# The attention gate of a diffusion transformer block: from TensorE to VectorE, ScalarE and GpSimd

## Chip, core and metric

One core of a Trainium2 chip. Its engines run their own instruction queues side by side and meet at semaphores: TensorE (matrix products, into PSUM), VectorE, ScalarE, GpSimd (element-wise work), and SyncE, which only issues transfers here. In profile rows they are PE, DVE, ACT, POOL and SP; PEld is TensorE's loading of weights. The metric is the device time of one execution in microseconds (us), the median over runs.

## What is computed

One block over two images of 256 tokens, D = 1152, two heads. A small vector c per image is turned into six vectors per image by `w_mod`: shift, scale and gate for the attention half and for the MLP half. The change concerns `gate_a`.

```python
mod = (_silu(c) @ w_mod).reshape(B, 6, 1, D)
shift_a, scale_a, gate_a, shift_m, scale_m, gate_m = [mod[:, i] for i in range(6)]
h = _layernorm(x, axis=-1) * (1 + scale_a) + shift_a
qkv = (h @ wqkv).reshape(B, N, 3, H, Dh)
...
attn = _softmax(jnp.einsum('bqhd,bkhd->bhqk', q, k) * Dh ** (-0.5), axis=-1)
a = jnp.einsum('bhqk,bkhd->bqhd', attn, v).reshape(B, N, D) @ wo
x = x + gate_a * a
h2 = _layernorm(x, axis=-1) * (1 + scale_m) + shift_m
m = _gelu(h2 @ w_fc1) @ w_fc2
return x + gate_m * m
```

All inputs are bf16; sums run in fp32.

## The kernel before

Tokens are four tiles of 128 (two per image). Contractions over D run over nine slices of 128 (`kt` 0 to 8). All SBUF is one tensor, `arena`, cut by byte offsets, so nearly every profile row names `arena` and `psum`, and several buffers share space over time. The stages in TensorE's order: layernorm and scale of x; k; `sh` (the shift vector, 36 narrow products); q; scores and softmax of the four (image, head) pairs, between the pieces of v; transposes of the probabilities; `rows` (three modulation vectors); the rest of v; probabilities times v (`PV`); `wo` with gate, residual and second layernorm; fc1 with gelu; fc2 with the second gate.

**Order.** The code records units with reads, writes and an estimated length. `Sched.schedule` (L281) fixes the order. TensorE (`pe`) and SyncE (`sp`) keep the order in which units are recorded. For VectorE, ScalarE and GpSimd a list scheduler runs the units with their estimated lengths and takes, of the units that are ready, the one with the longest chain behind it. `emit` (L398) writes one in-order queue per engine, with the semaphore waits that are still needed. An instruction that waits therefore holds up all that stand behind it on its engine. The estimates know nothing of engines that hinder each other.

**The attention gate before.** `ld_modr0`, `3` and `6` (L891-892) load 2592 KB each: for three kt, the 3 x 1152 columns of gate_a, shift_m and scale_m. They stand on SyncE's queue behind V's weights (`ld_wv`, L890), which wait until `sh` has freed their place. `rows` (L977) takes silu(c), two columns per kt, as the stationary operand, and streams the 27 x 128 columns in four groups of 32 columns side by side (`quad_mm`, L880): two sets of four instructions per kt, of 448 and 416 columns. ScalarE copies the gate part to bf16 `ROWS` (L982), VectorE transposes the rest into `MT` (L985), GpSimd's queue stores the gate to a scratch tensor in DRAM and loads it back spread over all 128 partitions as `GA[0]` and `GA[1]` (L988-992).

**Who reads it.** `wo_tile` (L1055): VectorE multiplies each finished PSUM piece by `GA[b]` (`wo_t1`, L1067), GpSimd adds x (`wo_x1`, L1068), VectorE takes the layernorm statistics (L731 and on), GpSimd the power -0.5 (L735), VectorE a product of two columns (`nmr2`, L1072), ScalarE normalises (`xn2`, L1073), TensorE transposes (`xn2_T`, L1078), and fc1 follows.

**The attention stage.** `q_kt0` to `q_kt8` (L1105) fill six PSUM banks, which `qk_ev` units copy out, on VectorE and ScalarE in turn; `S_halves` (L921) and `s_and_softmax` (L931) use those banks again. Per pair: scores on TensorE (`S_b_h`), `smax` and `snb` on VectorE (L943, L944), two `sexp` on ScalarE (L947), `sri` and the normalisation `spn` on VectorE (L949, L951), whose number is 2b + h. `pt_transposes` (L953) needs `spn`, and `PT_ev` copies its result out. V's pieces (`v_t_ci`, L965) use three banks in turn, copied out by `v_ev`.

**The MLP gate** is already made off TensorE: `mlp_gate` (L994) runs 18 multiply-adds on VectorE (weights times a per-partition scalar plus accumulator, L999 and L1002), a transpose in blocks of 32 (L1006), a reduction (L1008) and small moves and adds (L1011-1017).

Of the kernel before, what the change touches and what calls it, by code (L numbers as in the profile page):

```python
# [492 lines left out]
F32 = mybir.dt.float32  # L493
ALU = mybir.AluOpType
ACTF = mybir.ActivationFunctionType
AX = mybir.AxisListType

P = 128
NTOK = 512
D = 1152  # L500
KT = 9
# [16 lines left out]
def c_act(n, aps=0):  # L518
    return 190.0 + 0.8 * n + 75.0 * aps


def c_dve_psum32(n):
    return 110.0 + 1.13 * n


def c_dve_psum16(n):
    return 110.0 + 0.57 * n
# [14 lines left out]
def build_kernel(nc, x, c, wqkv, wo, w_mod, w_fc1, w_fc2, out):  # L542
    S = Sched()
# [3 lines left out]
    scratch = scratch_t.ap()  # L547
    with (
# [4 lines left out]
        def sb(off, nbytes, dt=BF16):  # L553
            assert off % 4 == 0 and off + nbytes <= ARENA_BYTES, (off, nbytes)
            v = arena[:, off // 2:(off + nbytes) // 2]
            if dt == F32:
                v = v.bitcast(F32)
            return v

        def ps32(bank, c0=0, n=512):  # L560
            return psum[:, bank * 512 + c0: bank * 512 + c0 + n]
# [7 lines left out]
        W1 = 20736  # L569
        O_A, O_B, O_C, O_R = 0, W1, 2 * W1, 3 * W1  # L570
# [10 lines left out]
        def misc(nbytes):  # L581
            o = mo[0]
            mo[0] += (nbytes + 3) // 4 * 4
            assert mo[0] <= ARENA_BYTES
            return o

        def wmat(o, f):
            return sb(o, KT * f * 2).rearrange("p (k f) -> p k f", k=KT)
# [7 lines left out]
        WMODR = wmat(O_R + W1, 3 * D)  # L596
# [18 lines left out]
        GA = [sb(O_GA + b * 2304, 2304) for b in range(2)]  # L615
        GM = [sb(o + 18432, 2304) for o in (O_A, O_C)]
        XN2 = [sb(O_R + 4 * W1 - (i + 1) * 2304, 2304) for i in range(4)]
        ROWS = sb(O_R + 4 * W1 - 5 * 2304, 2304)[:, 0:288]
        T1 = [sb(O_X + i * 1536, 1536, F32) for i in range(3)]
        OST = [sb(O_X + 4608 + i * 768, 768) for i in range(3)]  # L620
        gt_offs = ([O_P + i * 1024 for i in range(8)] + [O_B + i * 1024 for i in range(20)]
# [11 lines left out]
        ST32 = sb(misc(72), 72, F32)  # L633
# [4 lines left out]
        MT = sb(misc(2304), 2304, F32)  # L638
# [21 lines left out]
        wmod_v = w_mod.rearrange("(k p) f -> p k f", p=P)  # L660
# [4 lines left out]
        def dma(dst, src, nbytes, name, is_out=False, eng="sp", run=4096):  # L665
            eff = 1.0 if run >= 4096 else (1.08 if run >= 2304 else (1.15 if run >= 1536 else (1.3 if run >= 1024 else 1.42)))
            return S.op(eng, 500.0 if eng == "sp" else 150.0, lambda e: e.dma_start(dst, src), reads=[src], writes=[dst],  # L667
                        name=name, dma_bytes=nbytes * eff, is_out=is_out)

        def dve(cost, fn, reads, writes, name):  # L670
            return S.op("dve", cost, fn, reads=reads, writes=writes, name=name)

        def act(cost, fn, reads, writes, name):
            return S.op("act", cost, fn, reads=reads, writes=writes, name=name)

        def pool(cost, fn, reads, writes, name):
            return S.op("pool", cost, fn, reads=reads, writes=writes, name=name)

        def copy_on(eng, dst, src, n, psum16, name):
            if eng == "act":  # L680
                act(c_act(n), lambda e: e.activation(out=dst, in_=src, func=ACTF.Copy), [src], [dst], name)  # L681
            else:
                dve(c_dve_psum16(n) if psum16 else c_dve_psum32(n), lambda e: e.tensor_copy(dst, src), [src], [dst], name)  # L683

        def mm(o, l, r, st, sp, **kw):
            S.instr(lambda e: e.matmul(o, lhsT=l, rhs=r, start=st, stop=sp, **kw), reads=[l, r], writes=[o])  # L686
# [8 lines left out]
        for (ka, kb) in ((0, KC), (KC, KT)):  # L695
            w = (kb - ka) * P
# [49 lines left out]
        for t in range(4):  # L746
# [3 lines left out]
            else:  # L750
# [3 lines left out]
                                                                                 op0=ALU.subtract, op1=ALU.mult),  # L754
# [122 lines left out]
        def quads(w, g0, g1, q):  # L877
            return w.rearrange("p (g q c) -> p g q c", q=4, c=32)[:, g0:g1, q, :]

        def quad_mm(bank, w, g0, g1, kt):  # L880
            n = 32 * (g1 - g0)
            for q in range(4):
                o = psum[32 * q:32 * q + 2, bank * 512:bank * 512 + n].rearrange("p (g c) -> p g c", c=32)
                mm(o, ST[:, kt:18:9], quads(w, g0, g1, q), kt == 0, kt == KT - 1, tile_position=(0, 32 * q))
# [2 lines left out]
        S.unit("pe", KT * 4 * 31.0 + 100.0, "sh")  # L887
        for kt in range(KT):
            quad_mm(0, WSH[:, kt, :], 0, 9, kt)
        dma(WV, wqkv_v[:, :, 2 * D:3 * D], D * D * 2, "ld_wv", run=2304)  # L890
        for k0 in range(0, KT, 3):  # L891
            dma(WMODR[:, k0:k0 + 3, :], wmod_v[:, k0:k0 + 3, 2 * D:5 * D], 3 * P * 3 * D * 2, "ld_modr%d" % k0)
        MT1 = ps32(0, 0, 288)
        dve(c_dve_psum32(288), lambda e: e.transpose(SHA, MT1), [MT1], [SHA], "sha")  # L894
        for kt in range(KT):
            for b in range(2):
                src, dst = HK[:, kt, b * 256:(b + 1) * 256], HX[:, kt, b * 256:(b + 1) * 256]
# [74 lines left out]
            copy_on("act" if v_rr[0] % 2 else "dve", V[:, t, ci * CH:(ci + 1) * CH], o, CH, False, "v_ev%d_%d" % (t, ci))  # L972


        row_parts = ((3, 0, 14), (4, 14, 27))

        def rows():  # L977
            S.unit("pe", KT * 864 / 2.4 + 500.0, "rows")
            for kt in range(KT):
                for bank, g0, g1 in row_parts:  # L980
                    quad_mm(bank, WMODR[:, kt, :], g0, g1, kt)
            copy_on("act", ROWS, ps32(3, 0, 288), 288, False, "rows_ev")  # L982
            for i, (bank, c0, n, d0) in enumerate(((3, 288, 160, 0), (4, 0, 416, 160))):
                src, dst = ps32(bank, c0, n), MT[:, d0:d0 + n]
                dve(c_dve_psum32(n), lambda e, src=src, dst=dst: e.transpose(dst, src), [src], [dst], "mt_%d" % i)  # L985
            sc, so = MT[:, 288:576].rearrange("p (k r) -> p k r", r=32)[:, :, 0:2], SC1M.rearrange("p (k b) -> p k b", b=2)
            dve(170, lambda e: e.tensor_scalar(out=so, in0=sc, scalar1=1.0, scalar2=None, op0=ALU.add), [sc], [so], "sc1m")
            for b in range(2):  # L988
                dma(scratch[0, b].rearrange("(k q c) -> q k c", q=4, c=32), ROWS[b:128:32, :].rearrange("p (k c) -> p k c", c=32),
                    2304, "st_g%d" % b, eng="pool")  # L990
            for b in range(2):
                dma(GA[b], scratch[0, b].partition_broadcast(P), P * D * 2, "ld_g%d" % b, eng="pool")

        def mlp_gate(prev):  # L994
# [55 lines left out]
        def acc_bank():  # L1050
            b = acc[acc_rr[0] % len(acc)]
            acc_rr[0] += 1
            return b
# [47 lines left out]
            act(c_act(ntok), lambda e: e.activation(out=dst, in_=o, func=ACTF.Gelu_apprx_tanh), [o], [dst], "gelu_%d_%d" % (f, tok0))  # L1101


        qb = (2, 3, 4, 5, 6, 1)
        for kt in range(KT):  # L1105
            S.unit("pe", KG * c_mm(512), "q_kt%d" % kt)
# [21 lines left out]
        pt_transposes(1, 1)  # L1128
        v_proj(2, 0)
        rows()  # L1130
        wfc1_load(0)
        wfc1_load(1)
# [38 lines left out]
        for t in range(4):  # L1171
            b = t // 2
# [3 lines left out]
            for (c0, c1) in pieces:  # L1176
                w = c1 - c0
                S.unit("pe", JT * c_mm(w), "fc2_%d_%d" % (t, c0))
                o = ps32(acc_bank(), 0, w)
# [22 lines left out]
def bass_standalone__dit_block__diffusion_kernel(  # L1202
    nc: bass.Bass,
    x: bass.AP,
    c: bass.AP,
    wqkv: bass.AP,
    wo: bass.AP,
    w_mod: bass.AP,
    w_fc1: bass.AP,
    w_fc2: bass.AP,  # L1210
    out: bass.AP,
):
    build_kernel(nc, x, c, wqkv, wo, w_mod, w_fc1, w_fc2, out)
# [28 lines left out]
```

## Time and profile before

| | |
|---|---|
| median of three runs | 246.35 us (246.02 to 246.6) |
| the profiled execution | 246.26 us |
| its span, first to last instruction | 244.2 us |
| granted TensorE clock | 1.000 |
| TensorE busy | 239.3 us, 98% of the span |
| VectorE, ScalarE, GpSimd busy | 98.7, 63.0, 21.5 us |
| transfers | 51.57 MB |

The busy shares in 40 slices of 6.1 us, and what the transfers moved:

```profile
PE   7999999999999999999999999999999999999995
...
DVE  3742450446323689879999600000022222111112
ACT  5730340235312306983322333222000000000000
POOL 1400000000021275600000110000000000000000
DMA  6999999999994999979943589200000000000000
```

Each digit is the busy share in tenths. TensorE is full from the second slice to the last. GpSimd does nothing from slice 3 to slice 11, and VectorE is half idle there. In later fences a row of groups has line, engine, operation, shapes and count, then busy us and mean ns of one, then the idle time before it and what ended that. A row of a timeline has start, duration, engine, line, operation and count, and in brackets the idle time before it and its releaser.

### The profile page before, as it was taken

What the parts mean: (1) busy time and instruction counts of PE and PEld (TensorE: products, weight loads), DVE (VectorE), ACT (ScalarE), POOL (GpSimd) and SP (SyncE); (2) the same over time, 40 slices, a digit from 0 to 9 for tenths busy, and PEclk for the clock granted to TensorE, in tenths of its full rate; (3) what the DMA queues carried; (4) which work ended last, traced back from release to release, by engine and by line L of the source; (5) the groups of instructions that cost most, each with busy time, mean ns of one, the idle gap of its engine ahead of it and who ended that gap; (6) DMA issues with size and microseconds to landing.
All of it is one profiled execution on the core that took longest, in us unless ns stands there. A gap on an engine that the chain in (4) does not pass through costs nothing.

```text
span 244.2 us, 3973 instructions
## 1 busy us (share of the span) xinstructions
PE 239.3 (98%) x1721; PEld 146.8 (60%) x1731; DVE 98.7 (40%) x205; ACT 63.0 (26%) x128; POOL 21.5 (9%) x37
## 2 busy tenths in 40 slices
PE   7999999999999999999999999999999999999995
PEld 2689844466557666798544444444565656566575
DVE  3742450446323689879999600000022222111112
ACT  5730340235312306983322333222000000000000
POOL 1400000000021275600000110000000000000000
DMA  6999999999994999979943589200000000000000
GB/s 244 350 377 393 389 381 401 419 422 406 387 329 111 341 386 391 392 246 396 349 132 101 172 256 393 79 0 3 0 16 16 19 17 16 19 16 16 29 22 16
DMA packets 28875, 51.57 MB, mean 211 GB/s; under 512 B 1587, under 2 KB 15675, under 8 KB 28859
## 3 DMA queue, kind: packets, MB, share of 16 engines
q1 hardware_dynamic: 28384, 50.14, 56.9%
q0 software_dynamic: 448, 1.19, 2.0%
q8 instruction: 13, 0.21, 0.4%
q14 instruction: 3, 0.02, 0.0%
q10 hardware_dynamic: 27, 0.00, 0.0%
HBM read 50.14 MB, written 1.19 MB: 210 GB/s over the span
## 4 chain that ended last, share of the span: by engine, by line
PE 97%; ACT 1%; issue 0%; DVE 0%; POOL 0%; POOLq 0%
PE psum L686 95%; PE psum L689 2%; ACT arena L1091 1%; ACT arena L1073 1%; DVE arena L792 0%; POOL arena L709 0%; DVE arena L1184 0%; DVE arena L1185 0%; POOL arena L708 0%; DVE arena L783 0%; POOL arena L713 0%; POOLq L1227 0%
## 5 line engine op out<-in xcount | busy, mean ns | idle before, releaser
L686 PE MATMUL psum<-arena 128*128 128x384 bf16 (+9 forms) x1632 | 236.1, 312 | 2.2 <-POOL arena L709 1.4
L686 PEld LDWEIGHTS psum<-arena 128*128 128x128 bf16 (+1 forms) x1642 | 141.4, 97 | 92.3 <-issue 5.0
L1184 DVE TENSOR_TENSOR arena<-psum,arena 128x384 f32<-128x384 f32 (+3 forms) x14 | 7.0, 501 | 89.4 <-PE psum L686 89.4
L1101 ACT ACTIVATE arena<-psum 128x512 bf16<-128x512 f32 (+1 forms) x44 | 22.5, 522 | 42.6 <-PE psum L686 42.6
L681 ACT ACTIVATE arena<-psum 128x512 bf16<-128x512 f32 (+6 forms) x28 | 14.8, 549 | 40.1 <-PE psum L686 38.2
L683 DVE CAST arena<-psum 128x512 bf16<-128x512 f32 (+2 forms) x21 | 13.0, 627 | 26.5 <-PE psum L686 26.3
L1002 DVE SCALAR_TENSOR_TENSOR arena<-arena 128x1152 f32<-128x1152 bf16 x16 | 21.3, 1409 | 0.0
L1068 POOL TENSOR_TENSOR arena<-arena 128x384 f32<-128x384 f32 x12 | 11.0, 914 | 12.9 <-DVE arena L1067 11.7
L667 POOL DMA_DIRECT2D dit_scratch<-arena x4 | 2.6, 662 | 94.0 <-ACT arena L681 58.7
L731 DVE BATCH_NORM_STATS2 arena<-arena 128x6 f32<-128x384 f32 (+1 forms) x18 | 9.5, 549 | 1.2 <-DMA arena<-in_x_dram 1.1
L1073 ACT ACTIVATE arena<-arena 128x1152 bf16<-128x1152 f32 x4 | 5.4, 1353 | 9.5 <-DVE arena L1072 9.5
L1067 DVE TENSOR_TENSOR arena<-psum,arena 128x384 f32<-128x384 f32 x12 | 6.6, 548 | 3.2 <-PE psum L686 3.0
L689 PEld LDWEIGHTS psum<-arena 128*128 128x128 bf16 (+1 forms) x89 | 6.0, 98 | 2.4 <-DMA arena<-in_c_dram 0.8
L689 PE MATMUL psum<-arena 128*128 128x128 bf16 (+1 forms) x89 | 7.3, 219 | 0.1
L1185 DVE TENSOR_TENSOR arena<-arena 128x384 bf16<-128x384 f32 (+3 forms) x14 | 7.0, 501 | 0.5
L1091 ACT ACTIVATE arena<-psum,arena 128x128 bf16<-128x128 bf16 x16 | 6.1, 460 | 3.2 <-PE psum L689 2.5
L1088 DVE TENSOR_SCALAR arena<-psum,arena 128x128 bf16<-128x128 bf16 x20 | 5.5, 336 | 2.0 <-PE psum L689 1.8
L943 DVE TENSOR_REDUCE arena<-psum 128x2 f32<-128x512 f32 x4 | 2.8, 692 | 4.0 <-PE psum L686 3.7
L947 ACT ACTIVATE arena<-psum,arena 128x256 bf16<-128x256 f32 x8 | 3.7, 470 | 2.4 <-DVE arena L944 1.9
L735 POOL TENSOR_TENSOR arena<-arena 128x1 f32<-128x1 f32 x6 | 3.3, 555 | 6.1 <-DVE arena L734 6.1
L792 DVE TENSOR_SCALAR arena<-psum,arena 128x256 bf16<-128x256 bf16 x7 | 2.4, 348 | 3.6 <-PE psum L689 2.3
L900 ACT ACTIVATE arena<-arena 128x256 bf16<-128x256 bf16 x6 | 2.5, 495 | 3.3 <-DVE arena L894 3.3
(46 smaller groups left out, 43.1 us busy)
## 6 DMA issues: line engine op xcount, KB each, us to landing
arena<-in_w_mod_dram SPq DMA_DIRECT2D x4, 2592.0 KB, 20.2
arena<-in_w_fc_dram SPq DMA_DIRECT2D x9, 1152.0 KB, 8.2
arena<-in_w_fc_dram SPq DMA_DIRECT2D x4, 2592.0 KB, 17.4
arena<-in_wqkv_dram SPq DMA_DIRECT2D x18, 288.0 KB, 10.2
arena<-in_w_mod_dram SPq DMA_DIRECT2D x3, 864.0 KB, 13.2
arena<-in_wqkv_dram SPq DMA_DIRECT2D x1, 2592.0 KB, 10.9
arena<-in_wo_dram SPq DMA_DIRECT2D x1, 2592.0 KB, 32.7
arena<-in_w_mod_dram SPq DMA_DIRECT2D x3, 480.0 KB, 6.8
```

The lines of the kernel that those rows point to most:

```text
L681: act(c_act(n), lambda e: e.activation(out=dst, in_=src, func=ACTF.Copy), [src], [dst], name)
L683: dve(c_dve_psum16(n) if psum16 else c_dve_psum32(n), lambda e: e.tensor_copy(dst, src), [src], [dst], name)
L686: S.instr(lambda e: e.matmul(o, lhsT=l, rhs=r, start=st, stop=sp, **kw), reads=[l, r], writes=[o])
L689: S.instr(lambda e: e.transpose(o, i_, idn), reads=[i_, idn], writes=[o])
L731: dve(550, lambda e, s=s, o=o: e.bn_stats(out=o, in_=s), [s], [o], "bn_%s_%d" % (tag, ci))
L1002: u = dve(1300, lambda e, o=o, w=w, s1=s1: e.scalar_tensor_tensor(out=o, in0=w, scalar=s1, in1=o, op0=ALU.mult, op1=ALU.add), [w, s1, o], ...
L1068: S.op("pool", 930, lambda e, xs=xs, x1c=x1c: e.tensor_tensor(out=x1c, in0=x1c, in1=xs, op=ALU.add), reads=[x1c, xs], writes=[x1c], name=" ...
L1073: act(1344, lambda e: e.activation(out=xn2, in_=x1, func=ACTF.Identity, scale=rs, bias=nm), [x1, rs, nm], [xn2], "xn2_%d" % t)
L1091: act(440, lambda e, o=o, dst=dst, s1=s1, s2=s2: e.activation(out=dst, in_=o, func=ACTF.Identity, scale=s1, bias=s2), [o, s1, s2], [dst], ...
L1101: act(c_act(ntok), lambda e: e.activation(out=dst, in_=o, func=ACTF.Gelu_apprx_tanh), [o], [dst], "gelu_%d_%d" % (f, tok0))
L1184: dve(c_dve_psum32(w), lambda e, o=o, gm=gm, t1=t1: e.tensor_tensor(out=t1, in0=o, in1=gm, op=ALU.mult), [o, gm], [t1], "fc2_t1_%d_%d" % ( ...
L1185: dve(c_dve_32(w), lambda e, t1=t1, x1c=x1c, ost=ost: e.tensor_tensor(out=ost, in0=t1, in1=x1c, op=ALU.add), [t1, x1c], [ost], "fc2_out_%d ...
```

## The change

`gate_a` is no longer part of `rows`. Its weights are loaded by three transfers of their own (`ld_ga0`, `3`, `6`, 864 KB each), which stand ahead of V's weights on SyncE's queue; `ld_modr` shrinks to 1728 KB each. A new function `attn_gate`, recorded ahead of q, computes, with weights as bf16 and the accumulators as fp32 in a part of the arena that is free at that time:

- image 0: nine VectorE instructions of 128 x 1152 (`ga_0_kt`): one product, eight multiply-adds into `ACCA[:, 0]`;
- image 1: nine ScalarE products (`gp_kt`), the first into `ACCA[:, 1]`, the others in turn into two buffers; eight GpSimd adds (`ga_1_kt`) into `ACCA[:, 1]`;
- per image on VectorE a transpose (`ga_T`), a reduction (`ga_red`), three moves, three adds, a cast (`ga_bf`) and a small transpose (`ga_t`); then two stores on GpSimd's queue (`st_ga`), and at the end the load `ld_g` of `GA[b]` as before.

`ga_T0` writes into the buffer of odd products, so it waits for the GpSimd add of kt 7; `ga_T1` waits for that of kt 8. The buffers lie where the MLP gate's weights (`ld_gm`) come later, which now wait for the stores. `rows` keeps shift_m and scale_m: two sets of 288 columns per kt, and no copy on ScalarE.

```diff
-        ROWS = sb(O_R + 4 * W1 - 5 * 2304, 2304)[:, 0:288]
+        ACCA = sb(O_R, 9216, F32).rearrange("p (b d) -> p b d", b=2)
+        ACTA = sb(O_R + 9216, 9216, F32).rearrange("p (b d) -> p b d", b=2)
+        GPA = sb(O_R + 18432, 1152, F32).rearrange("p (q g) -> p q g", q=4)
...
+        for k0 in range(0, KT, 3):
+            dma(WMODR[:, k0:k0 + 3, 0:D], wmod_v[:, k0:k0 + 3, 2 * D:3 * D], 3 * P * D * 2, "ld_ga%d" % k0, run=2304)
         dma(WV, wqkv_v[:, :, 2 * D:3 * D], D * D * 2, "ld_wv", run=2304)
         for k0 in range(0, KT, 3):
-            dma(WMODR[:, k0:k0 + 3, :], wmod_v[:, k0:k0 + 3, 2 * D:5 * D], 3 * P * 3 * D * 2, "ld_modr%d" % k0)
+            dma(WMODR[:, k0:k0 + 3, D:3 * D], wmod_v[:, k0:k0 + 3, 3 * D:5 * D], 3 * P * 2 * D * 2, "ld_modr%d" % k0)
...
-        row_parts = ((3, 0, 14), (4, 14, 27))
+        row_parts = ((3, 9, 18), (4, 18, 27))
...
-            copy_on("act", ROWS, ps32(3, 0, 288), 288, False, "rows_ev")
...
+        def attn_gate():
+            for kt in range(KT):
+                o, w, s1 = ACCA[:, 0, :], WMODR[:, kt, 0:D], ST32[:, kt:kt + 1]
+                if kt == 0:
+                    dve(1300, lambda e, o=o, w=w, s1=s1: e.tensor_scalar(out=o, in0=w, scalar1=s1, scalar2=None, op0=ALU.mult),
+                        [w, s1], [o], "ga_0_%d" % kt)
+                else:
+                    dve(1410, lambda e, o=o, w=w, s1=s1: e.scalar_tensor_tensor(out=o, in0=w, scalar=s1, in1=o, op0=ALU.mult, op1=ALU.add),
+                        [w, s1, o], [o], "ga_0_%d" % kt)
+                s1 = ST32[:, 9 + kt:10 + kt]
+                o = ACCA[:, 1, :] if kt == 0 else ACTA[:, kt % 2, :]
+                act(c_act(D, 1), lambda e, o=o, w=w, s1=s1: e.activation(out=o, in_=w, func=ACTF.Copy, scale=s1), [w, s1], [o], "gp_%d" % kt)
+                if kt > 0:
+                    a_ = ACCA[:, 1, :]
+                    pool(3000, lambda e, o=o, a_=a_: e.tensor_tensor(out=a_, in0=a_, in1=o, op=ALU.add), [a_, o], [a_], "ga_1_%d" % kt)
+            pool(100, lambda e: e.memset(GBA, 0.0), [], [GBA], "gba0")
+            lin = scratch[0].rearrange("b (g c) -> b g c", c=32)
             for b in range(2):
...
+                a_, t_ = ACCA[:, b, :], ACTA[:, 1 - b, :]
+                gp, gb, gt = GPA[:, :, 36 * b:36 * b + 36], GBA[:, 64 * b:64 * b + 64], GTA[:, 64 * b:64 * b + 64]
+                dve(1400, lambda e, a_=a_, t_=t_: e.transpose(t_, a_), [a_], [t_], "ga_T%d" % b)
+                t3, o = t_.rearrange("p (g r) -> p g r", r=32), gp[:, 0, :]
+                dve(1400, lambda e, t3=t3, o=o: e.tensor_reduce(out=o, in_=t3, axis=AX.X, op=ALU.add), [t3], [o], "ga_red%d" % b)
...
+                dma(lin[b, 0:32], gt[:, 0:32], 2048, "st_ga%d_0" % b, eng="pool")
+                dma(lin[b, 32:36], gt[0:4, 32:64], 256, "st_ga%d_1" % b, eng="pool")
                 dma(GA[b], scratch[0, b].partition_broadcast(P), P * D * 2, "ld_g%d" % b, eng="pool")
...
+        attn_gate()
         qb = (2, 3, 4, 5, 6, 1)
```

On the queues the change has these places. VectorE: `ga_0_0` to `ga_0_4` before the copies of q (`qk_ev2`, `4`, `0`, `6`), `ga_0_5` and `ga_0_6` before `smax_0` and `qk_ev8`, `ga_0_7` before `sri_0` and `spn_0`, `ga_0_8` before `sri_2`, `smax_3` and `spn_2`; then `spn_1`, `v_ev1_0`, `PT_ev0`, `ga_T0`, `sri_3`, `v_ev1_2`, `spn_3`. GpSimd: the eight adds one after the other, then the stores and loads. ScalarE: four products before the copies of q, the others between copies and exps.

## The prediction

> **What bounds the kernel now.** I read the chain of waits first, then the groups by shape, then the timelines of GpSimd and VectorE. In the chain, whose shares are of the 244.2 us span, TensorE holds nearly everything:
>
> ```profile
> PE 97%; ACT 1%; issue 0%; DVE 0%; POOL 0%; POOLq 0%
> ```
>
> So work taken off TensorE is a gain of its full length, and work put on another engine is free until TensorE has to wait for it. From 45 to 65 us (attention) TensorE takes what VectorE makes. Starts and durations in us, VectorE and TensorE:
>
> ```profile
> 44.97 2.63 DVE L683 CAST arena<-psum 128x512 bf16<-128x512 f32 x4 [10.54 <-PE psum L686]
> 50.38 0.69 DVE L943 TENSOR_REDUCE arena<-psum 128x2 f32<-128x512 f32 x1 [2.77 <-PE psum L686]
> ...
> 61.68 0.69 DVE L951 TENSOR_TENSOR arena<-arena 128x512 bf16<-128x512 bf16 x1
> ...
> 64.19 0.39 PE L689 MATMUL psum<-arena 128*128 128x128 bf16 x4
> ```
>
> The casts free q's banks (S_halves follows at 48.8, S_0_0 at 49.3); L951 is the last softmax normalisation, spn_3, and at 64.19 TensorE transposes its result (PT_1_1). GpSimd is idle from 11.5 to 70.3 us, so nothing here shows what happens when GpSimd and VectorE work together. A later stage does:
>
> ```profile
> 95.05 0.92 POOL L1068 TENSOR_TENSOR arena<-arena 128x384 f32<-128x384 f32 x1
> ...
> 95.43 0.55 DVE L1072 SCALAR_TENSOR_TENSOR arena<-arena 128x1 f32<-128x1 f32 x1
> ...
> 99.34 0.91 POOL L1068 TENSOR_TENSOR arena<-arena 128x384 f32<-128x384 f32 x1
> ...
> 99.62 0.64 DVE L1072 SCALAR_TENSOR_TENSOR arena<-arena 128x1 f32<-128x1 f32 x1
> ...
> 103.44 0.16 DVE L1072 SCALAR_TENSOR_TENSOR arena<-arena 128x1 f32<-128x1 f32 x1 [0.66 <-POOL arena L735]
> ```
>
> One element per partition takes 0.16 us with GpSimd idle, but 0.55 and 0.64 beside a GpSimd add, ending at 95.98 and 100.26 where the adds end at 95.97 and 100.25 (a third, at 90.96, takes 0.63 and ends 0.01 after its add). This VectorE instruction reads two operands from SBUF. Those with one (L731, L1067, L1088) keep their length beside the same adds. I read an exclusive port: the second comer waits for the whole of the first. Each ga_0 multiply-add (weights and accumulator), each L951 and each new GpSimd add reads two operands from SBUF.
>
> **The change, part by part.**
>
> *TensorE.* The pass at lines 979-981 streams 864 columns per kt, starts at 65.97 and is followed at 69.36: 3.39 us. The pass with 288 columns (sh) has nine steps of 0.122 us, 1.1 us in all, so 576 columns take 2.2 to 2.3. Gain 1.1 us. The ScalarE eviction that goes (0.41 us) was in idle time.
>
> *Transfers.* The three 864 KB pieces of gate weights go ahead of V's on SP's queue, without a wait. V's 2592 KB landed at 42.4 (issue 31.47 plus 10.9) at about 390 GB/s, 6.7 us, so it began at 35.7; the pieces now land at 38.0, 40.2 and 42.5, and V's at 49.2. Its first use is at 53.0: 3.8 us of cover, beyond which a delay would count in full. The later loads carry the same total of bytes and keep their times. ld_gm now waits on SP for the gate's stores (about 91.5 us) with the fc2 loads behind it; the two fc1 loads ahead of it, 11.3 us of transfer in the old trace, cover this. Cost nothing.
>
> *Prices.* VectorE multiply-add 1.4 (L1002, 1409 ns). ScalarE product: between 1.15 (L739) and 1.35 (L1073), taken 1.2 as its input is bf16. GpSimd add of 1152: the same instruction at 384 takes 914 ns, so 2.74 if all scales; a GpSimd cast of 18 columns takes 0.19, so with that as fixed part 2.36; with the 0.56 of L735 (a power, 1 column) as fixed part 1.63. I take 2.6. GPSIMD Engine Reference, section 3.1, of the Trainium skill has 4497 ns for an fp32 add of 2048 elements; from that I estimate 2.53, and the sum would be 0.5 lower.
>
> *The stage, in the order that the planner writes for the changed kernel.* ga_0_0 to ga_0_2 run 38.0 to 41.5; gp_1 is done at 40.4, so add 1 waits at the port and has it next: the multiply-add behind must first see its predecessor's semaphore, and the same holds for GpSimd, so they alternate. Port: add 1 41.5-44.1, ga_0_3 -45.5, add 2 -48.1, ga_0_4 -49.5. Queued on VectorE behind ga_0_4 are the four q casts, 4.5 us late: S_halves 50.9, S_0_0 51.5 (+2.2). Port: add 3 -52.1, ga_0_5 -53.5, add 4 -56.1, ga_0_6 -57.5, add 5 -60.1. Behind ga_0_6 stand smax_0 and the cast qk_ev8, so S_0_1 starts at 58.9, not 54.46 (+4.4). Then ga_0_7 60.1-61.5, spn_0 61.8-62.5, add 6 -65.1, ga_0_8 -66.5, add 7 -69.1, spn_2 -69.8, add 8 -72.4, spn_1 -73.1. PT_1_0 waits for spn_2: 69.9, not 60.81 (+9). Then VectorE alone: v_ev1_0 0.56, PT_ev0 0.42, ga_T0 1.29 (half of L1006), sri_3 0.15, v_ev1_2 0.56, spn_3 0.69, with semaphores 76.7. PT_1_1 starts at 76.75 instead of 64.19: 12.55 us late.
>
> The account is simple: from 41.5 the port carries 8 adds (20.8), 6 multiply-adds (8.4) and 3 normalisations (2.1), 31.3 us and 0.3 idle, ending at 73.1. Which goes first moves the early stalls, not this sum; only if spn_1 gets in before add 8 is it 2.6 less. ScalarE's nine products (10.8 us) stay below it: by this count an exp waits at most 0.2 for one, and off the path.
>
> SBUF — State Buffer of the Trainium skill, section "Who interferes with whom", states this lock for a VectorE instruction with two SBUF inputs against a GpSimd one that reads SBUF, whole instructions long; the trace agrees at 384 columns and shows no longer one. By that rule the sum stands as it is; without it, see the first rival.
>
> *After the stage.* The reduction chain (two reduces 1.28, one transpose 1.29, 14 small ones near 0.2, L1011 and L1014) ends near 84.5 for image 0 and 86.5 for image 1. GpSimd issues four stores, the last to 87.9; they land about 4.2 after issue (the 2.2 KB stores at 70.3), image 0's by 89.5, and ld_g0 4.1 to 4.7 after its own: GA 0 is there at 93.5 to 94.2. Its first reader, wo_t1_0_0, moves from 82.71 to 94.2; ld_g1 behind it on GpSimd's queue waits for image 1's stores (91.5), and wo_x1, queued behind that, comes at 94.8. Cost nothing, though the cover is at most 0.7 us: the loads near 140 us took 7.1, and so late a GA 0 would cost up to 2 us, as xn2T_0 has only 1.2 to spare. All behind it is bound by TensorE and shifts as a whole.
>
> *Sum.* 246.26 (the profiled execution, 2.06 of it outside the span) + 12.55 - 1.1 = 257.7. The median, 246.35, is 0.1 above that execution: 257.8.
>
> **Rivals.**
>
> *No lock between long instructions* (the other side). It would show at 41.5, where add 1 and ga_0_3 would run together. Adds follow each other from 40.4 at 2.6 each; add 7 ends at 61.7, ga_T0 at 63.0, and no cast is late. What stays is that v_ev1_2 now stands ahead of spn_3: V's block ends at 64.19, the cast 0.56 and spn_3 0.69 follow, PT_1_1 starts at 65.5 (+1.3). 246.35 + 1.3 - 1.1 = 246.6, no change; 245.3 if even that is hidden. For it: no row has both long. Against it: three short ones out of three ended with the add. It decides where the overlap is over half of each add.
>
> *A lighter add.* At 1.63, eight adds are 7.8 shorter: 250.0. At 2.74, 258.9. With spn_1 ahead of add 8: 255.2.
>
> *A colder TensorE.* The 17 warm-up matmuls of 512 columns at the start take 0.38 each, later 49 take 10.74, 0.22 each. The longest new pause is 4.5 us, before PT_1_0. If it brings the slow pace back for as long as at the start (5.7 us), 5.7 x (1 - 0.22/0.38) = 2.4, partly hidden under the next wait: 259 to 260.2. Against it: the granted clock reads 1.00 in every window, so only matmul spacing would show it. TensorE: Matmul & The Clock Gate of the Trainium skill, Part 1, has the clock halved after an idle window of about 3.4 us that runs freely; a 4.5 us pause need not cover one.
>
> *A late gate vector*: +2, 259.8.
>
> **How the numbers follow.** The lock with adds of 2.36 to 2.74, either order: 0.67 (255 to 259). Lighter adds or a looser lock: 0.13 (249.5 to 255). Cold clock or late gate: 0.11 (259 to 262). No lock: 0.08; anything else 0.01. The range 250 to 261 leaves out the no-lock case and the ends of two others, under 0.2. About 0.2% (0.5 us) is what a measurement can tell from no change. No lock splits into same 0.05, faster 0.02 and slower 0.01, which with the rest gives slower 0.92; 0.01 more of faster is for what I overlook.
>
> **What would show it.** In the changed profile: GpSimd adds near 2.6 back to back with multiply-adds, each of which seems to last up to 4 us; L951 rows over 2 us; TensorE pauses before S_halves, S_0_1, PT_1_0, PT_0_1 and PT_1_1; the rows pass 2.2 us; wo_t1_0_0 waiting for TensorE, not a DMA. Multiply-adds of 1.4 beside adds of 2.6 that overlap them would make the forecast wrong.

## The result, and the profile after

The changed kernel takes 256.52 us (median of six runs, 255.43 to 256.94) where the kernel before takes 246.47 (six runs, 245.92 to 246.87): ratio 1.0405, 95% interval 1.0387 to 1.0422. The forecast was 257.8. The profiled execution took 256.89 us, its span is 254.8 (244.2 before), the mean granted clock 0.987.

The page of the changed kernel, the chain that ended last, as shares of the span:

```profile
PE 76%; DVE 13%; DMA 8%; ACT 1%; SPq 1%; issue 0%
```

TensorE held 97% of it before. VectorE now holds 13%. Of the 8% for transfers 11.45 us stand where that stretch begins: the first product, `ga_0_0` at 37.46, waits for its weights, and from there the chain runs through VectorE. What TensorE waited for (us in total, times, longest):

```profile
PE psum L693 <- DVE arena L957: 6.1, 2, 4.8
PE psum L690 <- DVE arena L687: 1.9, 2, 1.2
```

L957 is `spn` (L951 before), L687 the copies out of PSUM (L683 before). The timeline of TensorE has the places:

```profile
49.83 6.25 PE L690 MATMUL psum<-arena 64*128 64x256 bf16 x45 [0.68 <-DVE arena L687]
57.25 4.52 PE L690 MATMUL psum<-arena 128*128 128x256 bf16 x31 [1.17 <-DVE arena L687]
...
68.25 0.61 PE L693 MATMUL psum<-arena 128*128 128x128 bf16 x4 [4.80 <-DVE arena L957]
...
71.54 0.63 PE L693 MATMUL psum<-arena 128*128 128x128 bf16 x4
...
75.84 0.40 PE L693 MATMUL psum<-arena 128*128 128x128 bf16 x4 [1.25 <-DVE arena L957]
```

These are `S_halves` (48.75 before), the rest of `S_0_1` (54.78), `PT_1_0` (60.81), `PT_0_1` (62.50) and `PT_1_1` (64.19): +1.1, +2.5, +7.4, +9.0 and +11.65. Of the last, `rows` gives back 1.08 (2.31 us instead of 3.39), and 10.6 us is what the span grew by. GpSimd and VectorE in the same stretch, one timeline each:

```profile
39.94 18.52 POOL L1008 TENSOR_TENSOR arena<-arena 128x1152 f32<-128x1152 f32 x5 [28.54 <-ACT arena L1005]
61.21 9.46 POOL L1008 TENSOR_TENSOR arena<-arena 128x1152 f32<-128x1152 f32 x3 [2.74 <-ACT arena L1005]
```

```profile
41.23 3.65 DVE L1001 SCALAR_TENSOR_TENSOR arena<-arena 128x1152 f32<-128x1152 bf16 x1
...
57.11 1.38 DVE L950 TENSOR_SCALAR arena<-arena 128x2 f32<-128x2 f32 x1
...
59.01 1.40 DVE L1001 SCALAR_TENSOR_TENSOR arena<-arena 128x1152 f32<-128x1152 bf16 x1
...
60.41 0.14 DVE L950 TENSOR_SCALAR arena<-arena 128x2 f32<-128x2 f32 x1
60.52 0.69 DVE L957 TENSOR_TENSOR arena<-arena 128x512 bf16<-128x512 bf16 x1
...
65.76 2.44 DVE L957 TENSOR_TENSOR arena<-arena 128x512 bf16<-128x512 bf16 x1
...
68.19 2.50 DVE L950 TENSOR_SCALAR arena<-arena 128x2 f32<-128x2 f32 x1
70.61 0.68 DVE L957 TENSOR_TENSOR arena<-arena 128x512 bf16<-128x512 bf16 x1
```

Five adds follow each other every 3.70 us (18.52 / 5). A multiply-add takes 1.40 when GpSimd pauses (59.01) and 3.65 when an add is ahead of it; `spn` takes 0.69 or 2.44. Even `snb` (L950), two elements per partition, takes 0.14 or 2.50. Nobody is slower at the work; the second comer waits for the first. "The port" below stands for what the two engines lock against each other.

### The profile page after: what moved, and what is told of

The parts are those of the page before. It is cut to its first block, busy times and chain, and to the rows that moved or that the text cites. A ratio compares the mean times of both kernels' runs of the same rounds, so it can differ in the third digit from the quotient of the medians.

```text
span 254.8 us, 4051 instructions
## 1 busy us (share of the span) xinstructions
PE 241.8 (95%) x1731; PEld 147.3 (58%) x1731; DVE 130.4 (51%) x234; ACT 73.1 (29%) x136; POOL 49.4 (19%) x48
## 4 chain that ended last, share of the span: by engine, by line
PE 76%; DVE 13%; DMA 8%; ACT 1%; SPq 1%; issue 0%
PE psum L690 74%; DMA arena<-in_w_mod_dram 8%; DVE arena L1001 7%; PE psum L693 2%; DVE arena L957 1%; DVE arena L687 1%; DVE arena L950 1%; DVE arena L949 1%; ACT arena L1127 1%; SPq L671 1%; ACT arena L1109 1%; DVE arena L998 0%; DVE arena L796 0%; DVE arena L1221 0%; DVE arena L1222 0%
## 5 line engine op out<-in xcount | busy, mean ns | idle before, releaser
L690 PE MATMUL psum<-arena 128*128 128x384 bf16 (+7 forms) x1642 | 237.6, 311 | 4.0 <-DVE arena L687 1.9
L1008 POOL TENSOR_TENSOR arena<-arena 128x1152 f32<-128x1152 f32 x8 | 27.1, 3390 | 32.2 <-ACT arena L1005 31.3
L1038 DVE SCALAR_TENSOR_TENSOR arena<-arena 128x1152 f32<-128x1152 bf16 x16 | 21.4, 1415 | 0.0
L685 ACT ACTIVATE arena<-psum 128x512 bf16<-128x512 f32 (+5 forms) x27 | 14.2, 554 | 24.4 <-PE psum L690 20.9
L687 DVE CAST arena<-psum 128x512 bf16<-128x512 f32 (+2 forms) x21 | 12.9, 624 | 11.3 <-PE psum L690 11.2
L1001 DVE SCALAR_TENSOR_TENSOR arena<-arena 128x1152 f32<-128x1152 bf16 x8 | 18.0, 2253 | 0.2
L1005 ACT ACTIVATE arena<-arena 128x1152 f32<-128x1152 bf16 x9 | 11.1, 1255 | 6.8 <-POOL arena L1008 4.7
L671 POOL DMA_DIRECT2D dit_scratch<-arena x6 | 3.4, 570 | 49.1 <-DVE arena L1053 35.3
L953 ACT ACTIVATE arena<-psum,arena 128x256 bf16<-128x256 f32 x8 | 3.7, 472 | 11.2 <-DVE arena L950 11.2
L950 DVE TENSOR_SCALAR arena<-arena 128x2 f32<-128x2 f32 x4 | 5.7, 1419 | 0.0
```

The source lines that it names most:

```text
L1001: dve(1410, lambda e, o=o, w=w, s1=s1: e.scalar_tensor_tensor(out=o, in0=w, scalar=s1, in1=o, op0=ALU.mult, op1=ALU.add), [w, s1, o], [o], ...
L1005: act(c_act(D, 1), lambda e, o=o, w=w, s1=s1: e.activation(out=o, in_=w, func=ACTF.Copy, scale=s1), [w, s1], [o], "gp_%d" % kt)
L1008: pool(3000, lambda e, o=o, a_=a_: e.tensor_tensor(out=a_, in0=a_, in1=o, op=ALU.add), [a_, o], [a_], "ga_1_%d" % kt)
L1038: u = dve(1300, lambda e, o=o, w=w, s1=s1: e.scalar_tensor_tensor(out=o, in0=w, scalar=s1, in1=o, op0=ALU.mult, op1=ALU.add), [w, s1, o], ...
```

## The experiments

Ratios are to the kernel before, run beside it on the same chip (its median lay between 246.38 and 247.0), with 95% intervals. In every run but a1 the orders of VectorE, ScalarE and GpSimd are written out by hand; in e1 to e4b, e6, e8 and e10 they stand as in the changed kernel, but for the moves shown.

| kernel | us | ratio |
|---|---|---|
| e1 adds of 16 columns | 246.94 | 1.0025 (1.0014 to 1.0037) |
| e2 multiply-adds of 16 columns | 250.16 | 1.0165 (1.0150 to 1.0180) |
| e3 as e1, spn_3 ahead | 245.50 | 0.9966 (0.9956 to 0.9975) |
| e4, e4b idle matmuls in the pause | 256.50, 256.63 | 1.0424 (1.0408 to 1.0439), 1.0398 (1.0374 to 1.0421) |
| a1 the changed kernel again | 256.09 | 1.0394 (1.0363 to 1.0424) |
| e5 another split of the work | 249.21 | 1.0079 (1.0047 to 1.0110) |
| e6 adds in three pieces | 254.50 | 1.0314 (1.0291 to 1.0337) |
| e7 e5 mended | 247.88 | 1.0043 (1.0028 to 1.0059) |
| e8 e6, spn_3 ahead | 251.56 | 1.0186 (1.0152 to 1.0221) |
| e9 e7 mended | 245.34 | 0.9951 (0.9938 to 0.9965) |
| e10 changed kernel, spn_3 ahead | 255.11 | 1.0352 (1.0335 to 1.0368) |

### One side of the alternation made short: e1, e2, e3

e1: all instructions and waits stay, only the length of the GpSimd adds goes.

```diff
-                    a_ = ACCA[:, 1, :]
+                    a_, o = ACCA[:, 1, 0:16], o[:, 0:16]
```

> The changed kernel with its order of instructions kept, but each of GpSimd's eight adds covers 16 of 1152 columns; image 1's gate lacks the rest of the sum. Port theory: with the adds short nothing blocks VectorE; the multiply-adds take 1.41 us each one after the other, the normalisations 0.69; the only pause left is the one before PT_1_1, since v_ev1_2 stands ahead of spn_3 (1.3 us), and rows gain 1.1: 246.6 us, between 246.0 and 247.5. Rival, the added work itself (18 operations more on VectorE, nine products on ScalarE, V's weights later) makes attention late: still 251 us or more.

Measured 246.94, as expected, with `PT_1_1` at 65.71. All but some 0.6 us of the loss of 10 hangs on the adds' length. The lock works the other way round too; GpSimd's timeline of e1:

```profile
47.88 1.24 POOL L1008 TENSOR_TENSOR arena<-arena 128x16 f32<-128x16 f32 x1 [3.85 <-ACT arena L1005]
50.79 0.22 POOL L1008 TENSOR_TENSOR arena<-arena 128x16 f32<-128x16 f32 x1 [1.66 <-ACT arena L1005]
```

The same 16 columns take 0.22 alone and 1.24 behind a multiply-add that had begun at 47.63.

e2: the same for VectorE's multiply-adds, the adds whole.

```diff
-                    dve(1410, lambda e, o=o, w=w, s1=s1: e.scalar_tensor_tensor(out=o, in0=w, scalar=s1, in1=o, op0=ALU.mult, op1=ALU.add),
-                        [w, s1, o], [o], "ga_0_%d" % kt)
+                    o, ws = o[:, 0:16], w[:, 0:16]
+                    dve(1410, lambda e, o=o, w=ws, s1=s1: e.scalar_tensor_tensor(out=o, in0=w, scalar=s1, in1=o, op0=ALU.mult, op1=ALU.add),
+                        [ws, s1, o], [o], "ga_0_%d" % kt)
```

> The changed kernel with its order kept and the eight adds whole, but VectorE's eight multiply-adds cover 16 of 1152 columns; image 0's gate lacks the rest. Port theory: adds of 2.5 us follow each other without pause, VectorE's short two-operand operations and its scalings (snb) still wait for the add that runs, the normalisations above all; by hand PT_1_1 is 5 us late: 250.4 us, between 249 and 252. Rival, the long multiply-adds load VectorE too much and the adds are harmless: 246.6 us.

Measured 250.16, as expected. VectorE's timeline of e2, then GpSimd's group of rows from 36 to 76 us:

```profile
40.21 0.23 DVE L1002 SCALAR_TENSOR_TENSOR arena<-arena 128x16 f32<-128x16 bf16 x1 [0.97 <-DMA arena<-in_w_mod_dram]
40.66 2.35 DVE L1002 SCALAR_TENSOR_TENSOR arena<-arena 128x16 f32<-128x16 bf16 x1 [0.21 <-DVE arena L1002]
...
60.18 2.55 DVE L957 TENSOR_TENSOR arena<-arena 128x512 bf16<-128x512 bf16 x1
```

```profile
L1009 POOL TENSOR_TENSOR arena<-arena 128x1152 f32<-128x1152 f32 x8 | 21.2, 2655 | 32.5 <-ACT arena L1006 31.6
```

A multiply-add of 16 columns takes ten times its length beside an add and ends 0.03 us behind it (43.01 and 42.98); so it is a wait, not shared bandwidth. And the adds, now nearly unhindered, show their own price: 2.66 us in the mean, 2.62 without the one that waited for `spn_2`. Adds alone cost 3.45 us against e1 (1.0165 - 1.0025, times 246.4); the long multiply-adds beside them another 5.9.

e3: e1 with `sri_3` and `spn_3` ahead of `ga_T0` and `v_ev1_2` on VectorE.

```diff
- ... PT_ev0 ga_T0 sri_3 v_ev1_2 spn_3 PT_ev1 ...
+ ... PT_ev0 sri_3 spn_3 ga_T0 v_ev1_2 PT_ev1 ...
```

> As the first run (adds of 16 columns), with sri_3 and spn_3 ahead of ga_T0 and v_ev1_2 on VectorE. If the pause before PT_1_1 comes from v_ev1_2 standing ahead of spn_3, it goes: 1.3 us less than the first run, 245.3 us, which is below the kernel before by the gain of the rows pass alone (1.1). If that pause has another cause: as the first run.

Measured 245.50, 0.9 below the kernel before. With short adds the queue's order costs 1.45 us (1.0025 - 0.9966), and what is left without port and order is the gain of the shorter rows pass. Together: -0.8 for the rows, 1.45 for the order, 3.45 for the adds beside attention, 5.9 for the long multiply-adds beside them. These are the steps of one chain of ratios, so that they add up to the loss of 10 by construction; taken away in another order, a part can have another size (e10 has the order at 1.0 to 1.3).

### The half clock: e4, e4b, a1

In the changed kernel's windows (busy time of each engine with its count, granted clock as PEclk, then the transfers) the clock falls in the pause before `PT_1_0`; a second profile of the same kernel, a1, beside it:

```profile
66.00:72.00 6.00, 3.75 (x18) 2.18 (x19) 6.00 (x6) 1.74 (x6) 4.52 (x2) 0.60 1.09 354
72.00:76.00 4.00, 2.75 (x14) 1.28 (x13) 2.79 (x6) 0.76 (x2) 0.00 (x0) 0.75 0.37 122
```

```profile
66.00:72.00 6.00, 3.37 (x18) 1.90 (x19) 6.00 (x6) 1.76 (x5) 4.89 (x2) 0.72 1.09 355
72.00:76.00 4.00, 2.68 (x22) 1.51 (x19) 4.00 (x8) 1.58 (x5) 0.00 (x0) 1.00 0.40 131
```

In the first the clock read 0.50 from 67.16 to 73.99, and `v_1_1` and `v_1_2` (nine matmuls each, 1.46 us in the kernel before) both run slow, 2.9 and 2.6 us. In a1 it read 0.50 from 68.10 to 71.51, and only `v_1_1` runs slow. e4 and e4b (the same kernel) keep TensorE busy in the pause:

```diff
+        for i in range(22):
+            S.unit("pe", 215.0, "warm_f_%d" % i)
+            mm(ps32(7), IDENT, Q4B, True, True)
         pt_transposes(1, 0)
```

> The changed kernel with 22 idle matmuls of 512 columns (4.75 us at full clock, into a free bank) on TensorE ahead of PT_1_0, where it paused 4.8 us. Theory: the pause made the granted clock fall to a half for about 4 us, and this costs 1.1 us of the loss: granted clock 1.00 from 62 to 76 us, v_1_1 1.5 us instead of 2.9, in all 255.3 us, and less spread between executions. Rival, the slower matmuls were hidden behind waits for VectorE anyway: 256.5 us.

> The changed kernel once more, unaltered, as the reference of its own chip and hour for e4b_warm_fill: 256.5 us (255.9 to 257.0) by every theory; PT_1_1 some 11.6 us later than in the kernel before.

> The same kernel as e4_warm_fill, now beside the unaltered changed kernel on the same chip. Theory: the pause of 4.8 us before PT_1_0 costs not only itself but some 1.2 us of half clock behind it (v_1_1 takes 2.9 us instead of 1.5); with 22 idle matmuls in the pause the run is 0.8 to 1.3 us below a1_after_again, about 255.4. Rival: the half clock is hidden under the wait for spn_3 that follows, PT_1_1 starts at the same time, and the two runs are equal within 0.4 us.

The edit did what it was to do: the clock read 1.00 in every window and `v_1_1` took 1.5 us. The time did not fall, a miss for the theory as I had put it. Times from `PT_1_0` to `PT_1_1` say more: 7.59 us in the changed kernel's profile, 6.27 in a1, 6.27 and 6.28 in e4 and e4b. TensorE's timeline of e4 shows why:

```profile
71.88 0.40 PE L693 MATMUL psum<-arena 128*128 128x128 bf16 x4 [1.23 <-DVE arena L957]
```

This is `PT_0_1`. At full clock TensorE waits 1.23 us there for `spn_1`; at half clock the longer `v_1_1` fills this wait (in a1 `PT_0_1` follows with no wait, and just as long after `PT_1_0`, 3.09 us). So a half clock that ends with `v_1_1` costs nothing; one that lasts through `v_1_2` costs 1.3, because `v_ev1_2`, which needs `v_1_2`, stands ahead of `spn_3`. The two stretches of half clock are 3.41 and 6.83 us long, one twice the other, and in a span of 254 us they make a mean clock of 0.993 and 0.987. The twelve runs of the changed kernel show these two values and divide by them: six with a mean clock of 0.986 or 0.987 have spans of 254.1 to 255.7 (mean 254.85), six at 0.993 have 253.3 to 254.2 (mean 253.7). What stays open is why the eight filled runs (254.0 to 255.1, mean 254.5) don't lie at 253.7. Their two profiles reach `S_halves` at 50.35 and 51.27, against 49.83 and 50.21, and two profiles each don't tell whether that is the edit's doing.

### The adds in pieces: e6 and e8

e6 cuts each add in three of 384 columns, the same sum.

```diff
-                    a_ = ACCA[:, 1, :]
-                    pool(3000, lambda e, o=o, a_=a_: e.tensor_tensor(out=a_, in0=a_, in1=o, op=ALU.add), [a_, o], [a_], "ga_1_%d" % kt)
+                    for j in range(3):
+                        a_, o_ = ACCA[:, 1, j * CH:(j + 1) * CH], o[:, j * CH:(j + 1) * CH]
+                        pool(1000, lambda e, o_=o_, a_=a_: e.tensor_tensor(out=a_, in0=a_, in1=o_, op=ALU.add), [a_, o_], [a_], "ga_1_%d_%d" % (kt, j))
```

> The changed kernel in its own order, with every GpSimd add cut into three of 384 columns (the same sum). Theory (the port passes to the engine that is waiting after each instruction): a VectorE instruction waits for one piece of about 0.9 us at most; the stalls on the path shrink, though the work to be done at the port is the same or a little more; 253 us (252 to 254.5). Rival: GpSimd's next piece needs no semaphore and is at the port at once, so it goes first and VectorE waits for all three; blocked instructions last as long as before (up to 3.6 us): 256.5 to 257.5.

Measured 254.50, at the upper edge of the theory's range (252 to 254.5). VectorE's timeline of e6:

```profile
41.39 2.03 DVE L1001 SCALAR_TENSOR_TENSOR arena<-arena 128x1152 f32<-128x1152 bf16 x1
...
63.50 0.81 DVE L957 TENSOR_TENSOR arena<-arena 128x512 bf16<-128x512 bf16 x1
...
64.32 0.88 DVE L950 TENSOR_SCALAR arena<-arena 128x2 f32<-128x2 f32 x1
...
69.54 1.38 DVE L1015 STREAM_TRANSPOSE arena<-arena 128x1152 f32<-128x1152 f32 x1 [2.95 <-POOL arena L1009]
```

The mechanism is the theory's: a blocked multiply-add takes 2.03 instead of 3.65, `snb` 0.88 instead of 2.50, so VectorE waits for one piece and has the port next, although GpSimd's following piece was ready. The size was not: at 69.54 `ga_T0` has waited 2.95 us for GpSimd's seventh add, whose operand lies where it writes, with `spn_3` behind it; `PT_1_1` comes at 72.07. e8 moves the order alone:

```diff
- ... PT_ev0 ga_T0 sri_3 v_ev1_2 spn_3 PT_ev1 ...
+ ... PT_ev0 sri_3 spn_3 v_ev1_2 PT_ev1 ga_T0 ...
```

> e6_split_adds (each GpSimd add in three pieces) with one thing moved: sri_3, spn_3 and the two copies behind them stand ahead of ga_T0 on VectorE. In e6 ga_T0 waited until 69.5 for GpSimd's seventh add, whose operand lies where it writes, and spn_3 stood behind it: PT_1_1 at 72.07, 4.3 us after v_1_2 had let TensorE go. Theory: that is an order, not the port; PT_1_1 comes near 67.8, and the run is 3.5 to 4.3 below e6: 250.2 to 251 where before reads 247.0. Rival: spn_3 is held up by the port or by its own inputs to nearly 72, and nothing is won: 254.

Measured 251.56, 3.2 us below e6 by the ratios, somewhat less than expected; `PT_1_1` came at 69.74, not 67.8. (The profile is of one of two runs at 252.1 and 252.6, with a mean clock of 0.993; the other two, at 1.000, took 250.5 and 251.0.) ScalarE's timeline of e8 has the rest:

```profile
66.37 1.25 ACT L1005 ACTIVATE arena<-arena 128x1152 f32<-128x1152 bf16 x1 [2.46 <-POOL arena L1009]
67.53 0.46 ACT L953 ACTIVATE arena<-psum,arena 128x256 bf16<-128x256 f32 x1
```

The product `gp_8` waited for GpSimd to free its buffer, and the exps of pair 3 (L953), which stand behind it on ScalarE, came 2.7 us late: `snb_3`, which they need, was done at 64.82. A third queue is bound to GpSimd here.

### The order in the kernel as it was changed: e10

The same move as in e8, with whole adds.

> The changed kernel with whole adds and one thing moved: sri_3, spn_3 and the two copies behind them ahead of ga_T0 on VectorE, as in e8. Theory (the port's account bounds PT_1_0 and PT_0_1, and only the last step, PT_0_1 to PT_1_1, is the order's): PT_1_0 stays near 68.4 and PT_0_1 near 71.6, PT_1_1 follows v_1_2 at once, near 73.4 (74.7 where the half clock lasts through v_1_2), and 1.1 to 1.5 us is won: ratio 1.033 to 1.036. Rival: more than the last step hung on it, and 3 us or more is won, as in the split kernel: ratio below 1.029.

Measured 255.11: `PT_1_0` 68.73, `PT_0_1` 71.82, `PT_1_1` 73.81, right behind `v_1_2`. The last step was the order's, 1.0 to 1.3 us of the loss (against a1, where the intervals just overlap, and against the first ratio). `PT_1_0` and `PT_0_1` kept their times within 0.5 us, as the port's account says.

### A version that beats both: e5, e7, e9

The gain of the rows pass can be had if GpSimd's adds are kept away from attention. In e5 VectorE makes all of image 0 and kt 0 to 5 of image 1, with the gate's weights loaded between the pieces of q's; GpSimd adds three times, after `spn_3`.

```diff
+            if kt % 3 == 2:
+                k0 = kt - 2
+                dma(WMODR[:, k0:k0 + 3, 0:D], wmod_v[:, k0:k0 + 3, 2 * D:3 * D], 3 * P * D * 2, "ld_ga%d" % k0, run=2304)
...
+                for b in range(2 if kt < 6 else 1):
+                    o, w, s1 = ACCA[:, b, :], WMODR[:, kt, 0:D], ST32[:, b * 9 + kt:b * 9 + kt + 1]
...
+            for kt, (o, to, t_) in ((6, (0, None, None)), (7, (1, 0, 1)), (8, (1, 0, 1))):
...
-                a_, t_ = ACCA[:, b, :], ACTA[:, 1 - b, :]
+                a_, t_ = ACCA[:, b, :], (sb(O_GA, 4608, F32), ACTA[:, 1, :])[b]
```

> A version meant to beat both; it computes everything. VectorE makes all nine multiply-adds of image 0 and the first six of image 1, in the places where it was idle before and in the middle of attention, with the normalisations ahead of them; the gate's weights are loaded between the pieces of q's; GpSimd adds only the three last products of image 1, and only after the last normalisation (spn_3), so that no GpSimd instruction stands beside attention. Theory (the port alone makes the loss): attention stays where it was, PT_1_1 at 64 to 65, the rows pass 2.3, total 245.3 to 246.2. Rival: the multiply-adds fill VectorE's gaps so far that casts and normalisations come late without any GpSimd add, or image 1's gate vector lands after its first use near 91: 247 to 250.

Measured 249.21, the rival's range, but not by the rival's mechanisms. (The profile is of one of two quicker runs, 247.67; the other four took 249.1 to 249.7 with a mean clock of 0.992 or 0.993, where the quicker two read 1.000, which points to a stretch of half clock in them; no trace shows what they waited for.) Attention kept its times (from `S_halves` to `PT_1_1` 15.43 us, 15.44 before). TensorE's waits in e5:

```profile
PE psum L690 <- DVE arena L687: 2.0, 1, 2.0
```

That wait is behind the stage, from 77.3 on, for `v_ev3_2`, which stood behind `ga_T1` and `ga_red1`, and these behind the three adds. e7 replaces one GpSimd add by a VectorE multiply-add and moves image 0's load from ScalarE's queue to GpSimd's:

```diff
-                for b in range(2 if kt < 6 else 1):
+                for b in range(2 if kt not in (6, 7) else 1):
...
-            for kt, (o, to, t_) in ((6, (0, None, None)), (7, (1, 0, 1)), (8, (1, 0, 1))):
+            for kt, (o, to, t_) in ((6, (0, None, None)), (7, (1, 0, 1))):
```

> e5_split_gate with its two late waits taken out; it computes everything. In e5 attention kept its times, but TensorE stood 2.0 us at 77.0 for the copy v_ev3_2, which stood on VectorE behind the transpose and the reduction of image 1, and those behind three GpSimd adds in a row (the last ended at 75.86); and ScalarE's queue was held from 70.0 to 74.8 by the load of image 0's gate, which waited there for its store. Now VectorE makes kt 0 to 5 and 8 of image 1, ScalarE only kt 6 and 7, GpSimd adds twice (end near 74), and that load waits on GpSimd's queue. Theory: no stall is left; before's time less 1.1 (the shorter rows pass), up to 0.5 lost to jitter: 245.4 to 246.2 where before reads 246.4 to 247.0, ratio 0.995 to 0.998. Rival: the multiply-adds that now stand between v's copies hold those up, or a gate vector comes late (needed near 82 and 91): 247 to 249.

Measured 247.88: a miss again, of the same kind. (ScalarE was not held from 70.0 in e5: the copy `v_ev2_2` ran there at 72.06, and the load waited from 72.55 to 74.84.) A wait of 1.2 us for `v_ev3_2` was left, and the load of image 1's gate, waiting on GpSimd's queue until 86.5 for its store, held up `wo_x1` there; TensorE's waits behind `wo` (0.5 and 0.2) were new. e9 takes these two:

```diff
- ... ga_1_5 v_ev2_1 ga_1_8 mt_0 ...
+ ... ga_1_5 ga_1_8 v_ev2_1 mt_0 ...
- ... ld_wfc1_2 ld_wfc1_3 ld_gm ...
+ ... ld_wfc1_2 ld_g1 ld_wfc1_3 ld_gm ...
```

> e7_split_gate2 once more, with the two waits that its trace still shows taken shorter; it computes everything. There v_ev3_2 came at 78.29, where TensorE wanted its bank at 77.0, because GpSimd's last add started only at 72.40, behind ga_1_8, and ga_1_8 behind a copy that waited for TensorE; and image 1's gate vector landed at 93.5, as its load (7 us) shared the queues with a piece of fc1's and the gate weights of the MLP. Now ga_1_8 follows ga_1_5 at once, and that load goes on SP's queue ahead of the fourth piece of fc1's weights. Theory: the stall falls from 1.2 to about 0.4, the vector lands before 88, and of the 1.1 us of the shorter rows pass 0.5 to 0.8 is left: ratio 0.996 to 0.998 (246.0 to 246.4 where before reads 246.9). Rival: copies and waits move elsewhere, ratio 1.000 to 1.004.

Measured 245.34 (244.97 to 245.61), ratio 0.9951 with an interval of 0.9938 to 0.9965, a little better than expected: it computes everything and is 1.2 us, half a per cent, below the kernel before. All that TensorE waits for in e9, both rows known from the kernel before, and two rows each of GpSimd's and VectorE's timelines:

```profile
PE psum L690 <- POOL arena L713: 1.5, 1, 1.5
PE psum L690 <- issue: 0.2, 1, 0.2
```

```profile
63.40 2.63 POOL L1010 TENSOR_TENSOR arena<-arena 128x1152 f32<-128x1152 f32 x1 [51.84 <-ACT arena L1007]
71.13 2.62 POOL L1012 TENSOR_TENSOR arena<-arena 128x1152 f32<-128x1152 f32 x1 [5.10 <-DVE arena L1003]
```

```profile
62.22 0.69 DVE L958 TENSOR_TENSOR arena<-arena 128x512 bf16<-128x512 bf16 x1
...
63.61 1.37 DVE L1018 STREAM_TRANSPOSE arena<-arena 128x1152 f32<-128x1152 f32 x1
64.90 0.52 DVE L687 CAST arena<-psum 128x384 bf16<-128x384 f32 x1
65.34 1.33 DVE L1020 TENSOR_REDUCE arena<-arena 128x36 f32<-128x1152 f32 x1
```

The first add starts at 63.40, behind `spn_3` (62.22, 0.69 long), and VectorE spends its 2.63 us on a transpose, a copy from PSUM and a reduction, all at their usual length.

## Why the prediction was right, step by step

**The bound and the mechanism.** Right. Add and multiply-add alternate from 41.2 on as forecast, one `L957` row passes 2 us (`spn_2`, 2.44), and TensorE pauses where it was said to, `PT_1_0` the longest (4.80; forecast 4.5). Only before `PT_0_1` is there no pause, as the half clock fills it; e4 has it, 1.23. e1, e2 and e6 tell the exclusive port from its rivals: *no lock* would leave 16 columns at 0.23 and not 2.35; *a lighter add* of 1.63 isn't there, an add alone takes 2.61 to 2.64; and `spn_1` did not get in before add 8, but came right after it. The reason given for the alternation, that each engine must first see its predecessor's semaphore, is not needed: in e6 the pieces of one add follow each other with no idle time, and the port still went to VectorE in between.

**The sizes on the port.** Too long, all but the idle time. In the alternation a period is 3.70, where 2.6 + 1.4 = 4.0 was put down. A multiply-add that had waited ended 1.22 after the add, not 1.4, which leaves 2.48 for an add. From 41.19 on the port carried the eight adds in 19.9 us (20.8 forecast), the six multiply-adds in 7.65 (8.4) and three `spn` in 1.85 (2.1), with 0.66 idle (0.3): the last `spn` on it ended at 71.29, where 73.1 was forecast. The early stalls were about half of what was forecast: `S_halves` +1.1 (2.1), the rest of `S_0_1` +2.5 (4.4).

**"Those with one SBUF operand keep their length."** Wrong as a rule. `snb` (L950), one operand in SBUF and two elements, took 2.50. It moved the sum little: `snb_0` waited out add 5, the reduction behind it came late, and the port stood idle for 0.55 before `ga_0_7`; `snb_3` waited out add 8, which `spn_1` behind it would have had to do as well. SBUF — State Buffer of the Trainium skill, "Who interferes with whom", lists copy, cast and tensor_scalar among the instructions that can take the shared ports, when their operands meet certain conditions, and says that a reduction never does on this chip; the rows of `snb`, and the reduction of 1.33 in e9, agree.

**VectorE alone, after the port.** 3.65 us from the last `spn` on the port to `PT_1_1` were forecast. In a1 it is 3.2 (71.66 to 74.90), in the changed kernel's profile 4.55 (71.29 to 75.84). The difference between the two is the half clock, which the prediction had as a rival with the late gate vector at 0.11, and argued against because the granted clock read 1.00 before. It came in every run of the changed kernel whose clocks were shown, and cost 1.1 to 1.3 in half of them, by the spans and by the step from `PT_1_0` to `PT_1_1`. TensorE: Matmul & The Clock Gate of the Trainium skill, Part 1, has half clock after an idle window of some 3.4 us; the pause of 4.80 with 0.50 behind it fits that, and the doubt I raised against it did not hold.

**The stage's sum.** `PT_1_1` 75.84 against 76.75: 1.8 less on the port, 0.9 more behind it, which is the clock.

**Rows pass.** 1.08 gained, 1.1 forecast. e3 shows 0.84 to 0.9 of it in the whole time.

**Transfers.** Right. V's weights landed at 49.05 (49.2 forecast), the gate's pieces at 37.44, 39.70 and 41.95, half a us earlier than put down. The small stores landed 1.5 to 1.8 after issue, not 4.2, `GA[0]` at 92.76, and `wo` started without a wait. That cover was thin, as said: in e7, where TensorE was 10 us further on, image 1's load, waiting on the same queue, cost.

**ScalarE.** "At most 0.2" was 0.4 to 0.5 (the exps of pair 2 began at 61.02 behind `gp_6`, their `snb_2` was done at 60.55); "off the path" held in the changed kernel. e8 shows how little was between: with the order mended and the adds in pieces, the exps behind `gp_8` were the next to be late, by 2.7 us.

**The total.** 246.26 + 11.65 - 1.08 = 256.83, the profiled execution 256.89, the median 0.4 below it, as two of the six runs have the shorter half clock and 0.993. That the total came so close (257.7 forecast for this execution) is in part luck: the port's account was 1.8 too long, and the half clock, which the sum left at nothing, made up for 1.3 of it.

## What to carry to other kernels

Work that is moved to an idle engine is free only if that engine shares nothing with the busy ones: look for short VectorE instructions that last as long as a GpSimd one beside them, and add up what both have to do on the port, not each engine's busy time. Keep long GpSimd instructions out of a stage in which TensorE waits for VectorE, put them beside transposes, reductions and copies from PSUM, or cut them in pieces. And look at what stands behind a waiting instruction on every in-order queue; of the loss here more than a microsecond was such an order, and e5, e7 and e8 had one more each.

## What the runs showed of the hardware that was not expected

- A `TENSOR_SCALAR` of 128 x 2 fp32, SBUF to SBUF, waits for a whole GpSimd add: 2.50 us instead of 0.14. In e5 three copies of 32 x 36 fp32 took 1.29 together beside the end of an add, 0.58 in e9 with GpSimd idle. A 32-block transpose of 1152 columns (1.37) and a reduction (1.33) don't wait. Nor does every `TENSOR_SCALAR` from SBUF to SBUF: this one (`sc1m`) ran in the middle of e9's add of 71.13 to 73.75. Its input takes two of every 32 columns; no run shows what makes the difference.

```profile
72.31 0.17 DVE L993 TENSOR_SCALAR arena<-arena 128x18 f32<-128x18 f32 x1
```

- A multiply-add that has waited at the port is 0.18 shorter behind it than one that starts freely (1.22 against 1.40); that part of its start lies in the wait is my reading, which no run tests.
- Between pieces of an add the port goes to the engine that waits, not to the next piece (2.03 for a multiply-add in e6).
- The granted clock fell to 0.50 at the pause of 4.80 us and came back after 3.41 us (68.10 to 71.51 in a1, 69.05 to 72.46 in e10) or after twice that (67.16 to 73.99 in the changed kernel's profile). In e10 it fell only 0.32 us after TensorE had work again (68.73), and in e6 a pause of 4.15 was enough.
